# Small steps from VectorE to ScalarE, four trees for k's maximum, and new lists for every queue, in a fused attention and feed-forward kernel

## The chip, the core and the metric

The kernel runs on one core of a Trainium2 chip. A core has TensorE (PE in the profile; its weight loads are PEld), VectorE (DVE), ScalarE (ACT), GpSimd (POOL) and SyncE (SP), each with an instruction queue of its own that it works off in order. An instruction starts when those before it on its engine allow it and the semaphores it waits for are there. Matrix products land in PSUM, in banks that VectorE and ScalarE read (GpSimd doesn't here); all else is in SBUF. Sixteen DMA engines move data; transfers are issued from SP's and POOL's queues, and POOL's are those that convert f32 to f16 on the way.

The metric is the device time of one execution in microseconds (us), the median of several runs.

## The reference

```python
# attention, 8 batches x 8 heads x 576 tokens x 64
q_s = exp(q - max(q, axis=-1));  q_s = q_s / (sum(q_s, axis=-1) + 1e-9)
k_s = exp(k - max(k, axis=2));   k_s = k_s / (sum(k_s, axis=2) + 1e-9)     # axis 2: tokens
kv  = einsum('bhsd,bhse->bhde', k_s, v)
att = einsum('bhsd,bhde->bhse', q_s, kv)
x   = att as (4608, 512)
# feed-forward
out = ((x @ w1) * (x @ w2)) @ w3 @ w_out      # w1, w2: 512x1024; w3: 1024x1024; w_out: 1024x512
```

## The kernel before, in words

**Steps and lists.** The kernel is a set of small named steps, and `Plan.run` (line 48) emits them in the order of one long list, `ORDER` (line 77). Each engine's queue is that list with the other engines' steps left out. A second list, `PICKS`, says for each step that can run on more than one engine which one takes it; `HW`, `LOADS` and `LATE` give the order of the loads from SP, from POOL, and from SP after those. The planner's rings (line 175) are buffers that a step takes and another gives back: `pab` 4 PSUM banks, `po` 2, `att` 2, `osb` 4 and `bsb` 4 in SBUF. `FILL` puts matmuls on zeros before named steps.

`LINKED = 350`: among the first 350 steps, those marked as port steps (the subtractions, the multiplication of q, the trees, some casts; on VectorE or GpSimd) also wait for each other in the order of the list, whenever the engine changes from one to the next.

**Names.** A name's first number is the batch b (for up, bs, ab, down, os and st: the chunk c of 512 tokens; 9 chunks, the last one holding the 64 tokens that each batch leaves over).

- Start: `w3t`, `w3T`, `pf`, `W3O` fold w3 and w_out into one 1024x512 matrix, in 8 parts: transpose on TensorE, copy out (one 1024-column copy), two halves of 4 matmuls each, scaled copy out. w3.0 to w3.3 are loads of one row of w3's blocks, w3.4 and w3.5 of two; wo.0 and wo.1 are w_out's halves. w3t.2 needs w3.2; w3t.4 and w3t.5 need w3.4; w3t.6 and w3t.7 need w3.5.
- k: `kmx` is the maximum over the 9 tokens that a partition holds: two reductions of 1152 elements (line 484), or a tree of four elementwise maxima (lines 493 to 496) in batches below `TREES`. `cb` is the maximum over partitions: a 32x32 transpose, a reduction, an exchange of maxima between neighbouring quarters of 32 partitions (four reductions of 32x8, line 506), a reduction over the pair, a transpose back. `ksub` subtracts, `kexp` takes the exponential (ScalarE).
- `kv`: the products of k and v on TensorE into both `att` banks, with the sum of k's exponentials in a last column. `kv2` adds epsilon to those sums (line 559, once for each of 2 groups), takes the reciprocal, multiplies.
- q, in two parts of 1024 and 1280 elements for a partition: `qmx`, `qsub`, `qexp`, `qsm`, `qeps`, `qrc`, `qn` (maximum, subtract, exponential, sum, epsilon, reciprocal, multiply). Then q is transposed: in batches 0 and 1 on TensorE (`qt`, copied out by `qT`), from batch 2 on by a DMA transpose from SP (`qd`, line 629).
- `xm`, `xt`: q times kv on TensorE (8 of 9 token groups, then the ninth); `xs`, `xts` copy them out. In batches 2 and later xm needs both parts of q.
- Feed-forward: `up.1` (w2) and `up.0` (w1) into a `pab` bank each, 0.87 us; `bs` copies the w2 product to SBUF on ScalarE or VectorE; `ab` multiplies (VectorE), which frees the w1 bank. `down` is 8 matmuls with the folded matrix, 1.73 us, the last ones of which need the last `ab` of their tokens; `os` copies out, `st` stores (two DMAs from SP).

Chunks 0 and 1 are worked in halves of 256 tokens: up.1.c.s.u has the half s and a pair of the 8 blocks of columns u.

Of the kernel before, what the change touches and what calls it, by code (L numbers as in the profile page):

```python
# [77 lines left out]
q.0.1 q.0.0 qmx.0.1 qsub.0.1 w3.3 w3.4 qexp.0.1 qmx.0.0 wo.0 wo.1 k.0 ident qsub.0.0 qexp.0.0 w3t.3  # L78
w3t.4 w3t.5 w3T.3 qsm.0.1 w3T.4 qeps.0.1 qrc.0.1 w3.0 w3.1 pf.3.0 qn.0.1 pf.4.0 qt.0.16 pf.3.1 W3O.3
w3T.5 pf.4.1 qt.0.8 w3.5 v.0 w3.2 q.1.0 qT.0.8 W3O.4 pf.5.0 w3t.0 k.1 w3T.0 pf.5.1 w2.0 W3O.5 w3t.1  # L80
pf.0.0 qT.0.16 w3T.1 pf.0.1 W3O.0 w3t.7 w3T.7 pf.1.0 w3t.6 pf.7.0 pf.1.1 w1.0 qsm.0.0 qeps.0.0
kmx.0.0 cb.0 ksub.0.1 kexp.0.1 w1.1 ksub.0.0 qrc.0.0 kexp.0.0 kv.0 qn.0.0 kv2.0 w3t.2 pf.7.1 qt.0.0
w2.1 qmx.1.0 W3O.1 w3T.6 k.2 W3O.7 w3T.2 pf.6.0 w2.2 qT.0.0 xm.0.0 xs.0.0.1 qsub.1.0 w1.2 qexp.1.0
kmx.1.0 pf.6.1 pf.2.0 pf.2.1 xs.0.0.0 xm.0.1 xs.0.1.0 xs.0.1.1 up.1.0.0.0 up.0.0.0.0 up.1.0.1.0
bs.0.0.0 up.0.0.1.0 up.1.0.0.1 w2.3 qsm.1.0 qeps.1.0 ab.0.0.0 qrc.1.0 w1.3 up.0.0.0.1 cb.1 qn.1.0
v.1 ksub.1.0 q.1.1 ksub.1.1 qt.1.0 W3O.2 bs.0.1.0 ab.0.1.0 up.1.0.1.1 up.0.0.1.1 bs.0.0.1 W3O.6
qT.1.0 bs.0.1.1 ab.0.0.1 q.2 v.2 kmx.2.0 ab.0.1.1 xt.0 kexp.1.0 up.1.0.0.2 bs.0.0.2 up.0.0.0.2
up.1.0.1.2 up.0.0.1.2 kmx.2.1 ab.0.0.2 cb.2 ksub.2.0 ksub.2.1 xts.0.0 xts.0.1 up.1.0.0.3 up.0.0.0.3
# [6 lines left out]
down.0.3 qn.2.1 qT.1.8 xm.1.1 vc.3.0 xs.1.1.1 xs.1.1.0 q.4 down.1.0 qd.2.0 kmx.3.0 qd.2.1 qmx.3.0
xt.1 vc.3.1 up.1.1.1.0 up.0.1.1.0 up.1.1.1.1 bs.1.1.0 up.0.1.1.1 up.1.1.1.2 xts.1.0 bs.1.1.1 os.1.0
xts.1.1 kmx.3.1 ab.1.1.0 os.0.3 qmx.3.1 xm.2.0 qsub.3.0 qmx.4.1 ab.1.1.1 qsub.3.1 qsub.4.1
up.0.1.1.2 down.1.1 xs.2.0.1 bs.1.1.2 k.4 st.0.1 v.5 v.4 st.0.2 xs.2.0.0 xm.2.1 xs.2.1.1 xs.2.1.0
up.1.1.1.3 up.0.1.1.3 up.1.2.0.0 bs.1.1.3 qexp.3.1 ab.1.1.2 cb.3 ksub.3.0 ksub.3.1 up.0.2.0.0
ab.1.1.3 kmx.4.0 bs.2.0.0 qexp.3.0 q.5 qsm.3.1 os.1.1 qexp.4.1 qsm.3.0 qeps.3.0 ab.2.0.0 qeps.3.1  # L100
qrc.3.1 qn.3.1 qd.3.1 st.1.0 qsm.4.1 kexp.3.1 up.1.2.0.1 bs.2.0.1 up.0.2.0.1 down.1.2 down.1.3
os.1.3 up.1.2.0.2 up.0.2.0.2 bs.2.0.2 qrc.3.0 ab.2.0.1 qn.3.0 kexp.3.0 up.1.2.0.3 ab.2.0.2
up.0.2.0.3 kmx.4.1 bs.2.0.3 kv.3 qd.3.0 up.1.2.0.4 ab.2.0.3 up.0.2.0.4 vc.5.0 vc.5.1 vc.4.1 vc.4.0
k.5 st.1.3 st.0.3 st.1.1 v.6 v.7 bs.2.0.4 kv2.3 os.1.2 up.1.2.0.5 ab.2.0.4 st.1.2 up.0.2.0.5
bs.2.0.5 qmx.4.0 xt.2 xm.3.1 xts.2.0 up.1.2.0.6 xts.2.1 ab.2.0.5 qsub.4.0 xs.3.1.1 xm.3.0 bs.2.0.6
xt.3 up.0.2.0.6 xts.3.1 xs.3.0.0 cb.4 up.1.2.0.7 xts.3.0 xs.3.0.1 up.0.2.0.7 xs.3.1.0 bs.2.0.7
ab.2.0.6 up.1.3.0.0 ksub.4.0 qexp.4.0 ab.2.0.7 down.2.0 kmx.5.1 bs.3.0.0 down.2.1 ksub.4.1 kexp.4.0
qmx.5.1 up.0.3.0.0 os.2.0 up.1.3.0.1 qsub.5.1 kexp.4.1 ab.3.0.0 down.2.2 qmx.5.0 bs.3.0.1 kmx.5.0
qsub.5.0 up.0.3.0.1 qeps.4.1 up.1.3.0.2 up.0.3.0.2 qrc.4.1 os.2.1 ab.3.0.1 qn.4.1 up.1.3.0.3 qsm.4.0
k.6 st.2.1 down.2.3 bs.3.0.2 qeps.4.0 ab.3.0.2 qexp.5.1 qd.4.1 up.0.3.0.3 qrc.4.0 qn.4.0 bs.3.0.3  # L110
st.2.0 up.1.3.0.4 qsm.5.1 kv.4 bs.3.0.4 ab.3.0.3 up.0.3.0.4 qd.4.0 qexp.5.0 os.2.2 up.1.3.0.5
ab.3.0.4 q.6 st.2.2 up.0.3.0.5 kv2.4 bs.3.0.5 qeps.5.1 up.1.3.0.6 os.2.3 qrc.5.1 ab.3.0.5 qn.5.1
up.0.3.0.6 st.2.3 bs.3.0.6 xm.4.0 ab.3.0.6 xm.4.1 xs.4.0.0 xt.4 up.1.3.0.7 xs.4.1.1 up.0.3.0.7
xs.4.1.0 bs.3.0.7 xs.4.0.1 ab.3.0.7 down.3.0 cb.5 down.3.1 os.3.0 xts.4.1 st.3.0 xts.4.0 kmx.6.0
ksub.5.0 up.1.4.0.0 os.3.1 down.3.2 bs.4.0.0 st.3.1 q.7 kmx.6.1 ksub.5.1 qd.5.1 up.0.4.0.0 kexp.5.0
up.1.4.0.1 qsm.5.0 up.0.4.0.1 bs.4.0.1 ab.4.0.0 qeps.5.0 up.1.4.0.2 kexp.5.1 ab.4.0.1 up.0.4.0.2
qrc.5.0 bs.4.0.2 qmx.6.1 qn.5.0 up.1.4.0.3 os.3.2 vc.6.0 up.0.4.0.3 st.3.2 ab.4.0.2 up.1.4.0.4
qmx.6.0 bs.4.0.3 qd.5.0 k.7 kv.5 bs.4.0.4 ab.4.0.3 qsub.6.0 up.0.4.0.4 vc.6.1 kv2.5 up.1.4.0.5
# [5 lines left out]
os.4.1 qrc.6.0 kv.6 ab.5.0.2 qn.6.0 xt.5 up.1.5.0.3 qsm.7.0 xts.5.0 os.4.2 up.0.5.0.3 xts.5.1
kmx.7.0 qsub.7.1 bs.5.0.3 qd.6.0 up.1.5.0.4 up.0.5.0.4 st.4.1 bs.5.0.4 ab.5.0.3 up.1.5.0.5 ab.5.0.4
st.4.0 up.0.5.0.5 bs.5.0.5 kv2.6 up.1.5.0.6 st.4.2 ab.5.0.5 xm.6.0 bs.5.0.6 xm.6.1 st.3.3 xt.6
up.0.5.0.6 xs.6.1.1 cb.7 xts.6.1 xts.6.0 up.1.5.0.7 xs.6.1.0 xs.6.0.0 up.0.5.0.7 xs.6.0.1 ab.5.0.6
down.4.3 ksub.7.1 qexp.7.1 bs.5.0.7 ab.5.0.7 up.1.6.0.0 os.4.3 qsm.7.1 vc.7.1 down.5.0 ksub.7.0
bs.6.0.0 qeps.7.1 up.0.6.0.0 qrc.7.1 up.1.6.0.1 ab.6.0.0 kexp.7.0 down.5.1 os.5.0 qeps.7.0 st.5.0
# [12 lines left out]
st.7.1 ab.8.0.5 up.0.8.0.6 bs.8.0.6 st.5.3 down.7.2 ab.8.0.6 st.6.3 up.1.8.0.7 up.0.8.0.7 os.7.2
bs.8.0.7 st.7.2 down.7.3 ab.8.0.7 down.8.0 os.7.3 st.7.3 down.8.1 os.8.0 st.8.0 down.8.2 os.8.1
st.8.1 down.8.3.0 os.8.2 down.8.3 st.8.2 os.8.3.0 st.8.3.0 os.8.3 st.8.3
# [764 lines left out]
```

## Time and profile before

| | us |
|---|---|
| median of 3 runs (lowest, highest) | 242.14 (242.06, 242.51) |
| the profiled execution | 242.07 |
| its span | 240.3 |
| TensorE busy | 232.4 |
| VectorE busy | 182.0 |
| ScalarE busy | 118.5 |
| GpSimd busy | 110.2 |
| first matmul of up | 34.58 |
| last matmul of TensorE ends | 237.0 |

The span is what the profile covers; 1.8 us of the execution lie outside it. TensorE's 232.4 us hold 9.2 us of matmuls on zeros. Busy us of each engine by stretch, from the trace:

| stretch | PE | DVE | ACT | POOL |
|---|---|---|---|---|
| 0 to 30 | 26.6 | 20.7 | 14.5 | 15.4 |
| 30 to 60 | 28.8 | 28.2 | 18.1 | 21.0 |
| 60 to 80 | 20.0 | 18.7 | 15.1 | 15.8 |
| 80 to 100 | 20.0 | 19.2 | 15.1 | 15.6 |
| 100 to 120 | 20.0 | 17.0 | 10.8 | 12.2 |
| 120 to 140 | 20.0 | 18.8 | 10.8 | 13.4 |
| 140 to 160 | 20.0 | 19.3 | 11.5 | 10.9 |
| 160 to 180 | 20.0 | 14.5 | 10.7 | 6.1 |
| 180 to the end | 57.0 | 25.7 | 11.9 | 0.0 |

A group of instructions in the profile has: line, engine, operation, what it writes and reads, count, busy us and mean ns of one, then the idle time of the engine just before them and who ended it. A row of the timeline has start, length, and in brackets the idle time before it.

### The profile page before, as it was taken

To read this page: it belongs to the slowest core of one execution; us is meant where nothing else is said; L and a number is where in the kernel's file an instruction comes from. 1 tells how busy PE (TensorE), PEld (TensorE's weight loads), DVE (VectorE), ACT (ScalarE), POOL (GpSimd) and SP (SyncE) were. 2 spreads that over 40 slices of the span, in tenths; PEclk is the share of its full clock that TensorE was granted. 3 is DMA by queue.
4 is the path that set the end of the run, shared out by engine and by line. 5 is a ranking of instruction groups with operands and counts; after the bars stand their busy time and mean duration, and the time that the engine had idled before them with its cause. 6 is when DMAs were issued, how large, how long until landed. Compare 5 with 4: busy or idle time off the path is not lost.

```text
span 240.3 us, 4954 instructions
## 1 busy us (share of the span) xinstructions
PE 232.4 (97%) x1987; PEld 121.0 (50%) x1987; DVE 182.0 (76%) x306; ACT 118.5 (49%) x187; POOL 110.2 (46%) x73
## 2 busy tenths in 40 slices
...
PEclk9999999999999999999999999999999999999999
...
GB/s 203 217 305 209 324 222 296 235 393 391 314 261 277 402 217 194 323 372 284 206 232 213 260 125 0 57 151 68 65 124 87 46 0 0 0 132 1 131 131 131
DMA packets 37894, 45.66 MB, mean 190 GB/s; under 512 B 15984, under 2 KB 22384, under 8 KB 37872
## 3 DMA queue, kind: packets, MB, share of 16 engines
...
q8 instruction: 15, 0.25, 0.4%
q14 instruction: 7, 0.06, 0.1%
...
## 4 chain that ended last, share of the span: by engine, by line
PE 83%; DVE 6%; DMA 6%; issue 2%; POOL 1%; ACT 1%; DVEq 0%; POOLq 0%
PE pab L768 50%; PE po L790 23%; DMA k<-in_k_dram 6%; PE po L805 3%; PE pkv L540 2%; PE po L452 2%; PE xm L654 2%; DVE ab L783 1%; DVE k L515 1%; DVE km L484 1%; PE qtp L621 1%; POOL w L402 1%; PE po L654 1%; DVE mx L506 1%; DVE kmx L493 1%
## 5 line engine op out<-in xcount | busy, mean ns | idle before, releaser
L783 DVE TENSOR_TENSOR ab<-pab,bsb 128x512 f16<-128x512 f32 x72 | 48.7, 682 | 24.0 <-PE pab L768 19.7
L768 PE MATMUL pab<-x,w2sb 128*128 128x512 f16 (+1 forms) x320 | 66.0, 337 | 0.0
L768 PE MATMUL pab<-x,w1sb 128*128 128x512 f16 (+1 forms) x320 | 65.9, 337 | 0.0
L323 ACT CAST bsb<-pab 128x512 f16<-128x512 f32 x59 | 34.5, 587 | 54.3 <-PE pab L768 53.9
L790 PE MATMUL po<-W3O,ab 128*128 128x512 f16 x256 | 59.7, 379 | 1.2 <-DVE ab L783 1.2
L768 PEld LDWEIGHTS <-w1sb 128*128 128x128 f16 x352 | 33.9, 98 | 27.6 <-DMA w1sb<-in_moe_w_dram 0.2
L768 PEld LDWEIGHTS <-w2sb 128*128 128x128 f16 x352 | 33.4, 98 | 27.6 <-issue 1.3
L790 PEld LDWEIGHTS <-ab 128*128 128x128 f16 x256 | 24.7, 98 | 30.6 <-DVE ab L783 1.9
L515 POOL TENSOR_TENSOR k<-k,cb 128x1152 f32<-128x1152 f32 x12 | 31.4, 2636 | 14.9 <-DVE cb L511 8.4
L574 POOL TENSOR_TENSOR q<-q,qm 128x1024 f32<-128x1024 f32 (+1 forms) x14 | 29.7, 2125 | 12.8 <-DVE qm L569 12.7
L606 POOL TENSOR_TENSOR en<-eq,qr 128x1280 f16<-128x1280 f16 (+1 forms) x12 | 25.8, 2159 | 20.7 <-DVE qr L599 20.7
L484 DVE TENSOR_REDUCE km<-k 128x128 f32<-128x1152 f32 x12 | 25.9, 2166 | 0.0
L569 DVE TENSOR_REDUCE qm<-q 128x20 f32<-128x1280 f32 (+1 forms) x16 | 21.3, 1342 | 3.6 <-DMA q<-in_q_dram 3.6
L523 ACT ACTIVATE ek<-k 128x1152 f16<-128x1152 f32 x16 | 18.5, 1163 | 9.5 <-POOL k L515 8.8
L323 ACT COPY osb<-po 128x512 f32<-128x512 f32 (+1 forms) x22 | 12.7, 576 | 20.6 <-PE po L790 14.1
L323 DVE COPY osb<-po 128x512 f32<-128x512 f32 (+1 forms) x15 | 10.0, 668 | 15.4 <-PE po L790 9.7
L587 DVE TENSOR_REDUCE qr<-eq 128x20 f32<-128x1280 f16 (+1 forms) x16 | 21.3, 1341 | 0.5 <-ACT eq L582 0.5
L582 ACT ACTIVATE eq<-q 128x1280 f16<-128x1280 f32 (+1 forms) x16 | 18.8, 1174 | 5.6 <-POOL q L574 3.8
L452 PE MATMUL po<-wosb,w3T 128*128 128x512 f16 x64 | 15.5, 379 | 0.7 <-DMA wosb<-in_moe_w_out_dram 0.4
L327 ACT ACTIVATE x<-xm 128x512 f16<-128x512 f32 x18 | 10.4, 608 | 4.6 <-PE xm L654 4.6
L323 DVE CAST bsb<-pab 128x512 f16<-128x512 f32 x13 | 8.9, 687 | 2.8 <-PE pab L768 2.3
L350 PE MATMUL po<-zero 128*128 128x512 f16 x31 | 9.2, 458 | 1.6 <-DVE zero L345 1.6
...
## 6 DMA issues: line engine op xcount, KB each, us to landing
...
```

Source lines behind the costliest of these rows:

```text
L323: return [(nc.scalar.copy if eng == "ACT" else engine[eng].tensor_copy)(out=out, in_=in_)]
L452: nc.tensor.matmul(st["pf", ft], lhsT=st["w3T", ft][:, gt, :], rhs=wosb[:, gt, :], start=(gt == 0), stop=(gt == N_FT - 1))
L484: dve.tensor_reduce(out=st["km", b][:, two(hp), :], in_=kb[:, two(hp), :, :].rearrange("p h j d -> p h d j"), axis=AX.X, op=ALU.max)
L515: return [engine[eng].tensor_tensor(out=kb[:, two(hp), :, :], in0=kb[:, two(hp), :, :], in1=st["cb", b][:, two(hp), None, :].broadcast_to( ...
L569: dve.tensor_reduce(out=st["qm", b][:, :, j], in_=qb[:, :, j, :], axis=AX.X, op=ALU.max)
L574: return [engine[eng].tensor_tensor(out=qb[:, :, j, :], in0=qb[:, :, j, :], in1=st["qm", b][:, :, j, None].broadcast_to([P, HH, n, D]), op ...
L582: nc.scalar.activation(out=st["eq", b, p], in_=qb[:, :, j, :], func=AF.Exp)
L587: dve.tensor_reduce(out=st["qr", b][:, :, slice(*PARTS[p])], in_=st["eq", b, p], axis=AX.X, op=ALU.add)
L606: return [engine[eng].tensor_tensor(out=st["en", b][:, j, :, :].rearrange("p j h d -> p h j d"), in0=st["eq", b, p], in1=st["qr", b][:, :, ...
L768: nc.tensor.matmul(st["p", one, c, sub, u][:, a * (t1 - t0):(a + 1) * (t1 - t0)], lhsT=w[:, ct, fb * P:(fb + 1) * P], rhs=x()[:, ct, t0:t1 ...
L783: dve.tensor_tensor(out=st["ab", c][:, nf * u:nf * u + nf, t0:t1], in0=cut(st["p", 0, c, sub, u]), in1=cut(st["bsb", c, sub, u]), op=ALU.mult)
L790: nc.tensor.matmul(st["po", c, tb], lhsT=st["ab", c][:, ft, tb * P:(tb + 1) * P], rhs=W3O[:, ft, :], start=(ft == 0), stop=(ft == N_FT - 1))
```

## The change

Four things are changed together.

1. The exchange between quarters, in all 8 batches, becomes a step of its own on ScalarE. `cb` is split in three: `cba` (VectorE: transpose, reduction), `cbx` (ScalarE: four copies of 32x8), `cb` (VectorE: reduction, transpose).
2. The addition of epsilon to k's sums becomes a step `kve` on ScalarE (two activations of 128x2, from PSUM); `kv2` keeps the reciprocal and the products.
3. `TREES` goes from 2 to 4: batches 2 and 3 take the tree for kmx too, which is a port step.
4. `ORDER`, `PICKS`, `FILL`, `HW`, `LOADS` and `LATE` are new throughout: nearly every queue's order differs.

Steps by engine that differ in number, before and after:

| step | VectorE | ScalarE | GpSimd |
|---|---|---|---|
| bs | 13, 21 | 59, 51 | |
| os | 15, 9 | 22, 28 | |
| W3O | 0, 3 | 8, 5 | |
| w3T | 2, 3 | 6, 5 | |
| xs | 7, 6 | 25, 26 | |
| xts | 4, 5 | 12, 11 | |
| ksub | 4, 6 | | 12, 10 |
| qsub | 2, 3 | | 14, 13 |
| qn | 4, 3 | | 12, 13 |
| vc (cast of v) | | 6, 5 | 6, 7 |

```diff
-    TREES = 2
+    TREES = 4
...
-        def cb():
+        def cba():
             t = work.tile([P, nq, QD], F32, tag="kmq", name="kmq")
             dve.transpose(out=t.rearrange("p n c -> p (n c)"),
                           in_=st["km", b].rearrange("p h d -> p (h d)"))
-            m = work.tile([P, nq, 2], F32, tag="mx", name="mx")
-            dve.tensor_reduce(out=m[:, :, 0], in_=t, axis=AX.X, op=ALU.max)
+            st["mx", b] = work.tile([P, nq, 2], F32, tag="mx", name="mx")
+            dve.tensor_reduce(out=st["mx", b][:, :, 0], in_=t, axis=AX.X, op=ALU.max)
+
+        def cbx():
+            m = st["mx", b]
             for x in range(P // QD):
                 y = x ^ 1
-                dve.tensor_reduce(out=m[x * QD:(x + 1) * QD, :, 1],
-                                  in_=m[y * QD:(y + 1) * QD, :, 0:1], axis=AX.X, op=ALU.max)
+                nc.scalar.copy(out=m[x * QD:(x + 1) * QD, :, 1], in_=m[y * QD:(y + 1) * QD, :, 0])
+
+        def cb():
             e = work.tile([P, nq], F32, tag="mxe", name="mxe")
-            dve.tensor_reduce(out=e, in_=m, axis=AX.X, op=ALU.max)
+            dve.tensor_reduce(out=e, in_=st["mx", b], axis=AX.X, op=ALU.max)
...
+        def kve():
+            st["rc", b] = work.tile([P, G, NHP], F32, tag="rc", name="rc")
+            for gg in range(G):
+                nc.scalar.activation(out=st["rc", b][:, gg, :], in_=st["pkv", b, gg][:, :, D],
+                                     func=AF.Identity, bias=epst[:, 0:1])
+
         def kv2():
...
-            rc = work.tile([P, G, NHP], F32, tag="rc", name="rc")
-            for gg in range(G):
-                dve.tensor_scalar_add(out=rc[:, gg, :], in0=ps[gg][:, :, D], scalar1=EPS)
+            rc = st["rc", b]
             dve.reciprocal(out=rc, in_=rc)
...
-    "begin": 17, "w3t.4": 8, "pf.3.0": 6,
+    "begin": 17, "w3t.4": 8, "qt.0.0": 7,
...
-    ("q", 0, 1), ("q", 0, 0),
+    ("q", 0, 0), ("q", 0, 1),
...
-    ("w3", 3), ("w3", 4), ("wo", 0), ("wo", 1), ("k", 0), ("w3", 0), ("w3", 1), ("w3", 5), ("v",
-    0), ("w3", 2), ("q", 1, 0), ("k", 1), ("w2", 0), ("w1", 0), ("w1", 1), ("w2", 1), ("k", 2),
-    ("w2", 2), ("w1", 2), ("w2", 3), ("w1", 3), ("v", 1), ("q", 1, 1),
+    ("w3", 0), ("w3", 4), ("wo", 0), ("wo", 1), ("w3", 2), ("k", 0), ("w3", 5), ("w3", 3),
+    ("w3", 1), ("v", 0), ("q", 1, 0), ("k", 1), ("w2", 0), ("w1", 0), ("w2", 1), ("w1", 1),
+    ("w2", 3), ("w1", 2), ("w2", 2), ("k", 2), ("w1", 3), ("v", 1), ("q", 1, 1),
```

The new `ORDER` up to the end of batch 2's attention, without the steps before kv.0 on TensorE that the prediction names one by one:

```
w3t.7 w3t.6 w2.0 w1.0 w3t.3 w2.1 w1.1 cbx.0 W3O.2 w3T.7 w2.3 w1.2 w2.2 qT.0.8 qT.0.16 cb.0 pf.7.0 pf.7.1
ksub.0.1 ksub.0.0 w3T.3 pf.3.0 pf.3.1 kexp.0.1 w3t.1 kexp.0.0 k.2 kv.0 W3O.3 w3T.1 W3O.7 w3T.6 qmx.1.0
kve.0 kv2.0 pf.1.0 pf.6.0 xm.0.0 qsub.1.0 xs.0.0.0 xs.0.0.1 pf.6.1 pf.1.1 kmx.1.0 xm.0.1 qexp.1.0
...
bs.0.0.3 ab.0.0.3 down.0.0 xts.0.0 kexp.1.1 cba.2 ab.0.1.2 xts.0.1 cbx.2 cb.2 ksub.2.1 kv.1 kve.1
bs.0.1.3 kexp.2.1 os.0.0 down.0.1 ksub.2.0 v.2 up.0.0.1.3 kv2.1 qmx.1.1 xm.1.0 xs.1.0.0 xs.1.0.1 qsub.1.1
ab.0.1.3 down.0.2 up.1.1.0.0 up.0.1.0.0
...
up.0.1.0.2 kv.2 kve.2 ab.1.0.1 up.1.1.0.3 up.0.1.0.3 qn.1.1 qrc.2.0 kv2.2 qn.2.0 qeps.2.1 qt.1.16 qt.1.8
os.0.3 ab.1.0.2 bs.1.0.3 qrc.2.1 qn.2.1 st.0.0 k.4 qd.2.0 ab.1.0.3 qT.1.16 down.1.0 qmx.3.1 qT.1.8 qd.2.1
q.4 st.0.1 xm.1.1 down.1.1 xs.1.1.1 xs.1.1.0 xt.1 kmx.3.0 qmx.3.0 up.1.1.1.0 up.0.1.1.0 xts.1.1 xts.1.0 xm.2.0
```

More of the change, by code (lines that the diff above doesn't have):

```diff
@@ L77 @@
 ORDER = """
[L78 to L88, printed above, removed]
@@ L95 @@
[L95 to L106, printed above, removed]
@@ L107 @@
[L107 to L118, printed above, removed]
@@ L124 @@
[L124 to L129, printed above, removed]
@@ L142 @@
[L142 to L144 removed]
+q.0.0 q.0.1 w3.0 ident qmx.0.0 qsub.0.0 w3.4 wo.0 wo.1 w3.2 k.0 qmx.0.1 w3.5 w3.3 qexp.0.0 qsm.0.0
+qsub.0.1 w3t.0 qeps.0.0 w3t.4 qrc.0.0 w3t.5 w3T.0 w3.1 qn.0.0 qexp.0.1 w3T.5 qsm.0.1 qeps.0.1
+qrc.0.1 qn.0.1 qt.0.0 pf.0.0 pf.5.0 pf.0.1 w3t.2 pf.5.1 W3O.0 qT.0.0 v.0 kmx.0.0 q.1.0 k.1 cba.0
@@ new lines @@
+w3T.2 W3O.5 qt.0.8 qt.0.16 pf.2.0 pf.2.1 w3T.4 pf.4.0 pf.4.1 W3O.4 w3t.7 w3t.6 w2.0 w1.0 w3t.3 w2.1
+w1.1 cbx.0 W3O.2 w3T.7 w2.3 w1.2 w2.2 qT.0.8 qT.0.16 cb.0 pf.7.0 pf.7.1 ksub.0.1 ksub.0.0 w3T.3
+pf.3.0 pf.3.1 kexp.0.1 w3t.1 kexp.0.0 k.2 kv.0 W3O.3 w3T.1 W3O.7 w3T.6 qmx.1.0 kve.0 kv2.0 pf.1.0
+pf.6.0 xm.0.0 qsub.1.0 xs.0.0.0 xs.0.0.1 pf.6.1 pf.1.1 kmx.1.0 xm.0.1 qexp.1.0 xs.0.1.1 xs.0.1.0
+up.1.0.0.0 bs.0.0.0 up.0.0.0.0 up.1.0.1.0 up.0.0.1.0 up.1.0.0.1 qsm.1.0 qeps.1.0 qrc.1.0 ab.0.0.0
+cba.1 w1.3 v.1 q.1.1 qn.1.0 bs.0.1.0 up.0.0.0.1 qt.1.0 ab.0.1.0 up.1.0.1.1 up.0.0.1.1 cbx.1 cb.1
```

100 lines of the change are left out of this document (68 added, 32 removed), and 100 rows, old and new, of the table PICKS.

## The prediction

> **What bounds the kernel now.** I read the engine shares first, then what TensorE waited for, then its timeline around its longest wait, then the timelines of the loads and of VectorE beside it. From the page and from TensorE's waits:
>
> ```profile
> PE 232.4 (97%) x1987; PEld 121.0 (50%) x1987; DVE 182.0 (76%) x306; ACT 118.5 (49%) x187; POOL 110.2 (46%) x73
> ...
> PEclk9999999999999999999999999999999999999999
> ```
>
> ```profile
> PE po L350 <- DVE zero L345: 1.6, 1, 1.6
> PE po L790 <- DVE ab L783: 1.2, 1, 1.2
> PE w3t L440 <- DMA w<-in_moe_w_dram: 0.7, 2, 0.5
> ```
>
> TensorE is busy 97% at full clock, and its waits are few. The timeline (start, length, idle before) shows where:
>
> ```profile
> 12.67 1.89 PE L452 MATMUL po<-wosb,w3T 128*128 128x512 f16 x8
> ...
> 34.58 1.05 PE L768 MATMUL pab<-x,w2sb 128*128 128x256 f16 x8
> ...
> 50.37 0.60 PE L790 MATMUL po<-W3O,ab 128*128 128x512 f16 x2 [1.23 <-DVE ab L783]
> ...
> 229.90 7.09 PE L805 MATMUL po<-W3O,ab 128*128 128x512 f16 x40
> ```
>
> After 52 us there is no gap to 237.0; only what lies before 52 us can be won, and any new gap after it is a loss. Two things time that first part. One is the loads:
>
> ```profile
> 15.04 1.89 PE L452 MATMUL po<-wosb,w3T 128*128 128x512 f16 x8 [0.36 <-DMA wosb<-in_moe_w_out_dram]
> ...
> 18.02 1.23 DVE L493 TENSOR_TENSOR kmx<-k 128x1024 f32<-128x1024 f32 x1 [2.94 <-DMA k<-in_k_dram]
> ...
> 19.14 0.71 PE L440 MATMUL w3t<-ident,w 128*128 128x128 f16 x8 [0.46 <-DMA w<-in_moe_w_dram]
> ```
>
> They land one behind the other: k.0 3.0 us after wo.1, the next one-row part of w3 1.1 us after k.0. The other is VectorE, 85 to 100% busy in each 6 us from 30 to 60 us. The prices that the change turns on, from the groups of instructions:
>
> ```profile
> L484 DVE TENSOR_REDUCE km<-k 128x128 f32<-128x1152 f32 x12 | 25.9, 2166 | 0.0
> ...
> L506 DVE TENSOR_REDUCE mx<-mx 32x8 f32<-32x8 f32 x32 | 4.9, 153 | 0.6
> ...
> L559 DVE TENSOR_SCALAR rc<-pkv 128x2 f32<-128x2 f32 x16 | 1.7, 150 | 1.8 <-PE pkv L550 1.8
> ...
> L593 ACT ACTIVATE qr<-qr,epst 128x16 f32<-128x16 f32 x5 | 1.5, 310 | 2.9 <-DVE qr L587 2.9
> ```
>
> (busy us, mean ns, idle before). And from the view of L629, the DMA transposes of q:
>
> ```profile
> DMA to landing us min/median/max: 3.1/3.6/7.4
> ```
>
> **The change, part by part.** All times are of the one profiled execution: span 240.3 us, 242.07 us in all, 1.8 us outside the span; the median of the three runs is 242.14.
>
> *Loads off VectorE.* The 32 copies at L506 leave it (4.9 us), and the 16 additions at L559 (1.7). Batches 2 and 3 exchange four reductions (4 x 2.17) for two trees (1.23 + 0.69 + 0.42 + 0.43 and small gaps, 2.9 each): 2.9 less. The new lists give back eight bs, three W3O, one w3T, one xts, one qsub and two ksub and take six os, one xs and one qn: +6.3. Net 3 us less on VectorE, spread over the attention.
>
> *Loads on ScalarE.* Four copies of 32x8 for each batch and two additions of 128x2. An ACT copy takes 372 ns at 256 columns and 586 at 512, so about 165 at 8; two of the small L593 activations stand in 0.52 us where they follow each other. I take 0.75 us for the four copies (bounds 0.6, the same on VectorE, and 1.24, four times L593) and 0.55 for the two additions (0.23, the two at L559, to 0.62). With fewer bs, W3O, w3T, vc and more os ScalarE gets about 5 us more, on an engine that is half idle. The cost is the hop: cb was 2.3 us in one go and is now 0.9 + 0.75 + 0.65 with two handovers, and cbx stands in ScalarE's queue between evictions. Queued behind a cbx that waits for its cba are, batch by batch, W3O.2 (pf.7 waits for its bank), qT.1.0, kve.1, xs.2.1.1, xts.2.1, kve.4, bs.4.0.1 (ab.4.0.1 and up.0.4.0.3 wait for it) and bs.5.0.0.
>
> *Start.* POOL issues w3.0, the identity, w3.4, wo.0, wo.1, w3.2 and only then k.0. The DMA queues have q to move meanwhile, so the identity's 0.6 us costs nothing; w3.2 costs k.0 the 1.2 us of one part, so it lands at 19.25. The qsub that held POOL's later issues in the old order is on VectorE now; since the queues were never empty, that gains nothing. Fills are 32 for 31 (0.2 us, inside the wait for qn.0.0 and wo.0). Walking the queues: tree 19.25 to 22.1; cba 23.0; cbx 23.8; cb 24.5; two ksub 27.1; kexp.0.0 28.4; kv.0 28.45. TensorE, with w3t.2 at 16.3 (w3.2), w3t.7/6 at 21.75 (w3.5), pf.7 at 24.35 (behind W3O.2, which is behind cbx.0), reaches kv.0 at 28.45 as well: one more w3t, half a pf and a qt now lie before kv.0 (27.11 in the old order, after a wait of 0.4). From there 5.6 us are left: kv 1.25, pf.1 and pf.6 3.46, two xm with the gaps before them 0.9. kve (29.8 to 30.4, behind w3T.6) and kv2 (31.15) hide behind the two pf, to 31.4. So up.1.0.0.0 starts at about 34.05 instead of 34.58: **-0.5 us**.
>
> *Chunk 0.* VectorE is the chain here. From kv2.0 (31.15): qsub, tree, qsm and two small ones to 36.85; ab, cba.1, ab 39.0; cb.1 39.9 (0.25 wait for cbx.1); bs, ksub, ab, bs, ab, W3O, ab 44.9; tree of batch 2 47.7 (k.2 was moved behind all w2 and lands at 43.1; POOL's ksub.1.1, which the port order puts first, ends at 44.5); ab.0.0.3 48.35. TensorE needs that ab for the last two of the eight matmuls of down.0.0 at 48.9: the 1.23 us of the old order are gone. Next: cba.2, ab, cb.2 50.7 (0.2 wait for cbx.2), ksub.2.1 52.05, bs, kv2.1 53.4, qmx, ab.0.1.3 55.45. TensorE has put down.0.1 and up.0.0.1.3 before that; down.0.2 waits 0.35 for ab.0.1.3 and ends at 55.9. The old order has the same work done at 56.09 + 1.73 = 57.8. **-1.4, so -1.9 together.**
>
> *Batch 2.* Here it is given back. POOL's chain starts at the end of ksub.2.1, since the port order makes ksub.2.0 wait for it: 2.64 + 2.34 + 2.34 + 1.91 + 1.15 + 2.34 + 1.91 + 2.34 with small gaps, so qn.2.1 ends at 69.45, which is when it ended before. The transposes land 3.6 us later: 73.1. The old order reached xm.2.0 at 74.8 and didn't wait; the new one has less work ahead of it, comes at about 72.4 and waits 0.7. Before that up.0.1.0.3 waits 0.35 for ab.1.0.1. With xm.2.0 done at 73.45, the same work was done at 74.25 before (74.82, less 0.55 of work listed ahead of it there and not here): **+1.1, leaving -0.8**.
>
> *Rest.* The tree of batch 3 (69.75 to 72.6) ties POOL's vc.3.1 and qsub.3.0 behind it, which still leaves ksub.3.1 done at 83.2 for kv.3 at 86.8. Chunk 2 has up.1.3.0.0 at 98.55 against 99.27. From there VectorE is nearly full to 142 us, with margins of 0.3 to 1.1 us (down.3.0 needs ab.3.0.7 at 124.6, up.1.5.0.0 needs xs.5.0.0 at 142.6 and comes at 143.7). The POOL steps listed between up.1.3.0.0 and up.1.5.0.0 were 29 us by their rows and are 44 now, in the same 45 us; POOL begins them 4.8 us early; kv.5 and kv.6 have 8 us and more. Stores moved past q.6 and k.6 on SP still free osb before the os that need it. Allowing 0.1 for these: **-0.7 in all**. The last steps are the same (a 256-column ACT copy and a store).
>
> 242.07 - 0.7 = **241.4 us**.
>
> **Rivals.** (a) *The transposes of batch 2 land late.* Twelve of them took 3.1 to 7.4 us. POOL's chain ends no earlier than before while TensorE comes 2.4 us earlier, so each us over 3.6 is one us of the end. At 4.8 us it is slower than before by 0.5; at 7.4 it gives 245.2; 5.5, the middle, 243.3. For it: k.4 and q.4 load around them. Against it: the median. (b) *Small ScalarE steps cost 0.31 each*, as L593 does. cbx becomes 1.24, and cbx.0 lies on both ways to kv.0: +0.5, then 241.9, no change. Against it: the copy rows' 158 ns at no columns. The Trainium skill, ScalarE: Activation LUTs, Rules for kernel authors, speaks for (b): it budgets about 0.3 us for each ACTIVATE with a pointer bias besides the elements. L593 agrees at 310 ns; whether a plain copy pays it no row here shows. By the rule for copies too the sum would be 241.9. (c) *VectorE overruns in chunks 3 and 4.* I priced back-to-back steps at 0.09 less than their means (two ab in 1.28); if half of that is missing over some 60 steps, 2.7 us less 1.1 of margin come on top: 243.0. For it: no idle time in that list. (d) *The waits close up.* If VectorE and POOL run 1.5 us ahead of my walk, both waits vanish: 239.9. Against it: POOL's chain has no slack.
>
> **How the numbers follow.** From no change a measurement of this kernel can tell about 0.2%, 0.5 us, that is 241.66 to 242.62. Forecast 0.42 (of which 0.06 within 0.2%), (a) 0.20, (b) 0.14, (c) 0.12, (d) 0.12. Faster 0.36 + 0.12 = 0.48; same 0.06 + 0.14 = 0.20; slower 0.32. The range runs from 240.2, which cuts half of (d), to 243.3, which cuts half of (a) and a quarter of (c), 0.19 in all; the forecast's own is 240.9 to 241.9.
>
> **What would show it.** Right: first L768 matmul near 34.0; no wait of 1.2 us for ab at the first down; TensorE waits 0.5 to 1 us before the xm of batch 2 near 73; ACT copies of 32x8 near 0.17 us each; nothing after 100 us. Wrong: kv.0 later than 29, the gap near 73 over 2 us, or gaps on ab between 100 and 145.

## The result, and the profile after

The changed kernel takes 244.04 us (median of 4 runs, 243.87 to 244.72) against 242.27 (4 runs, 242.06 to 242.51) for the kernel before: a ratio of 1.0078, with a 95% interval of 1.0055 to 1.0101. It is slower by 1.8 us; 241.4 was forecast, and 243.3 was the upper end of the range. Its profiled execution took 244.17 us, with a span of 242.4.

Engine shares and granted clock, from the page of the kernel after:

```profile
PE 232.4 (96%) x1988; PEld 121.3 (50%) x1988; DVE 179.7 (74%) x270; ACT 123.1 (51%) x228; POOL 106.3 (44%) x72
...
PEclk9999999999999999999999999999999999999998
```

The loads moved between engines as costed: VectorE 2.3 us less (3 forecast), ScalarE 4.6 more (5 forecast). TensorE's work is the same; the last slice's 8 lies behind its last matmul. So the 2.1 us by which the span is longer are waiting, 0.7 of them behind TensorE's last matmul. Everything TensorE waited for, from the view of waits of the kernel after (total us, times, longest):

```profile
PE po L350 <- DVE zero L345: 1.6, 1, 1.6
PE po L662 <- DMA qT<-en: 1.2, 1, 1.2
PE w3t L440 <- DMA w<-in_moe_w_dram: 1.2, 3, 0.6
PE xm L662 <- DMA qT<-en: 0.6, 1, 0.6
PE po L452 <- ACT w3T L323: 0.5, 1, 0.5
PE pab L779 <- DVE bsb L323: 0.3, 1, 0.3
PE pab L779 <- DVE ab L794: 0.2, 1, 0.2
```

The wait for ab at the first down is gone; two waits for DMA transposes and two for VectorE are new. TensorE's timeline of the kernel after shows their places:

```profile
22.43 1.97 PE L440 MATMUL w3t<-ident,w 128*128 128x128 f16 x24 [0.32 <-DMA w<-in_moe_w_dram]
...
26.66 1.90 PE L452 MATMUL po<-wosb,w3T 128*128 128x512 f16 x8 [0.54 <-ACT w3T L323]
28.40 0.65 PE L440 MATMUL w3t<-ident,w 128*128 128x128 f16 x8
28.98 0.78 PE L544 MATMUL pkv<-v,ek 64*64 64x64 f16 x72
...
34.58 1.05 PE L779 MATMUL pab<-x,w2sb 128*128 128x256 f16 x8
...
48.43 1.89 PE L801 MATMUL po<-W3O,ab 128*128 128x512 f16 x8
...
73.37 0.41 PE L662 MATMUL xm<-qT,kv 64*64 64x512 f16 x4 [0.62 <-DMA qT<-en]
...
97.57 0.41 PE L662 MATMUL po<-qT,kv 64*64 64x512 f16 x4 [1.23 <-DMA qT<-en]
...
156.13 1.02 PE L779 MATMUL pab<-x,w2sb 128*128 128x512 f16 x4 [0.35 <-DVE bsb L323]
157.33 1.02 PE L779 MATMUL pab<-x,w1sb 128*128 128x512 f16 x4 [0.17 <-DVE ab L794]
...
231.25 7.09 PE L816 MATMUL po<-W3O,ab 128*128 128x512 f16 x40
```

The same work, after minus before: up.1.0.0.0 0.0 (34.58 both); end of down.0.2 -1.5 (56.28, 57.82); up.1.2.0.0 -0.6 (79.41, 79.97); up.1.3.0.0 +0.7 (99.93, 99.27); batch 5's first xm +0.6 (140.42, 139.86); batch 6's first xm +1.3 (162.60, 161.26); last down +1.35 (231.25, 229.90); end of the span +2.1. The kernel is ahead until 79 us, loses 1.2 us at batch 3's xm, 0.8 us near 156, and the rest behind the last matmul. The prices of the moved steps, from the groups of instructions of the kernel after:

```profile
L509 ACT COPY mx<-mx 32x8 f32<-32x8 f32 x32 | 6.3, 197 | 4.8 <-DVE mx L503 4.4
...
L561 ACT ACTIVATE rc<-pkv,epst 128x2 f32<-128x2 f32 x16 | 3.3, 259 | 4.3 <-PE pab L662 2.0 <-PE pkv L554 1.2 <-PE pkv L544 1.0
```

And who makes batch 3's transposes late. VectorE, GpSimd and SyncE's queue, from the timelines of the kernel after:

```profile
84.34 1.48 DVE L577 TENSOR_REDUCE qm<-q 128x20 f32<-128x1280 f32 x1
85.73 2.17 DVE L484 TENSOR_REDUCE km<-k 128x128 f32<-128x1152 f32 x1
87.83 0.26 DVE L607 RECIPROCAL qr<-qr 128x20 f32<-128x20 f32 x1
```

```profile
83.25 1.15 POOL L323 CAST v<-v 128x1152 f16<-128x1152 f32 x1
85.95 2.34 POOL L582 TENSOR_TENSOR q<-q,qm 128x1280 f32<-128x1280 f32 x1 [1.55 <-issue]
88.25 4.21 POOL L614 TENSOR_TENSOR en<-eq,qr 128x1280 f16<-128x1280 f16 x2
```

```profile
90.62 1.28 SPq L637 DMA_TRANSPOSE qT<-en  x1
91.99 1.36 SPq L827 DMA_DIRECT2D out_dram<-osb  x2
93.44 1.34 SPq L637 DMA_TRANSPOSE qT<-en  x1
```

qrc.3.1 stands on VectorE behind kmx.4.0 and runs at 87.83; GpSimd has idled 1.55 us (qsub.4.1 needs qmx.4.1, which ends on VectorE at 85.82) and then does qsub.4.1, for batch 4, ahead of batch 3's qn.3.1 and qn.3.0, which end at 92.46; two stores are issued between the two transposes. The kernel before began qn.3.1 at 86.56, 1.7 us sooner, and issued its first transpose at 88.92; two stores stood between the two transposes there too.

### The profile page after: what moved, and what is told of

It is laid out like the page before. It is cut to its first block, busy times and chain, and to the rows that moved or that the text cites. A ratio compares the mean times of both kernels' runs of the same rounds, so it can differ in the third digit from the quotient of the medians.

```text
span 242.4 us, 4971 instructions
## 1 busy us (share of the span) xinstructions
PE 232.4 (96%) x1988; PEld 121.3 (50%) x1988; DVE 179.7 (74%) x270; ACT 123.1 (51%) x228; POOL 106.3 (44%) x72
## 4 chain that ended last, share of the span: by engine, by line
PE 50%; DVE 18%; DMA 9%; issue 7%; ACT 7%; POOL 6%; DVEq 0%; ACTq 0%; POOLq 0%
PE pab L779 30%; PE po L801 13%; DMA k<-in_k_dram 6%; DVE ab L794 5%; DMA qT<-en 3%; PE po L816 3%; POOL en L614 2%; PE po L452 2%; DVE qr L595 2%; ACT eq L590 2%; DVE qm L577 2%; DVE k L519 2%; ACT mx L509 2%; POOL q L582 1%; ACT bsb L323 1%
## 5 line engine op out<-in xcount | busy, mean ns | idle before, releaser
L519 POOL TENSOR_TENSOR k<-k,cb 128x1152 f32<-128x1152 f32 x10 | 26.2, 2633 | 13.5 <-DVE k L519 10.4
L614 POOL TENSOR_TENSOR en<-eq,qr 128x1024 f16<-128x1024 f16 (+1 forms) x13 | 27.2, 2106 | 4.4 <-issue 1.2
L582 POOL TENSOR_TENSOR q<-q,qm 128x1280 f32<-128x1280 f32 (+1 forms) x13 | 27.7, 2143 | 2.6 <-issue 1.6
L577 DVE TENSOR_REDUCE qm<-q 128x16 f32<-128x1024 f32 (+1 forms) x16 | 21.2, 1336 | 3.5 <-DMA q<-in_q_dram 3.5
L595 DVE TENSOR_REDUCE qr<-eq 128x16 f32<-128x1024 f16 (+1 forms) x16 | 21.2, 1330 | 2.0 <-ACT eq L590 2.0
L590 ACT ACTIVATE eq<-q 128x1024 f16<-128x1024 f32 (+1 forms) x16 | 18.5, 1164 | 3.7 <-POOL q L582 2.2
L323 DVE CAST bsb<-pab 128x512 f16<-128x512 f32 x21 | 14.4, 687 | 3.9 <-PE pab L779 3.3
L484 DVE TENSOR_REDUCE km<-k 128x128 f32<-128x1152 f32 x8 | 17.2, 2154 | 0.0
L323 DVE COPY osb<-po 128x512 f32<-128x512 f32 x9 | 6.2, 685 | 7.2 <-PE po L801 7.2
L323 POOL CAST v<-v 128x1152 f16<-128x1152 f32 x7 | 9.2, 1314 | 4.1 <-DVE km L496 3.0
```

The costliest lines, as they stand in the source:

```text
L323: return [(nc.scalar.copy if eng == "ACT" else engine[eng].tensor_copy)(out=out, in_=in_)]
L519: return [engine[eng].tensor_tensor(out=kb[:, two(hp), :, :], in0=kb[:, two(hp), :, :], in1=st["cb", b][:, two(hp), None, :].broadcast_to( ...
L577: dve.tensor_reduce(out=st["qm", b][:, :, j], in_=qb[:, :, j, :], axis=AX.X, op=ALU.max)
L582: return [engine[eng].tensor_tensor(out=qb[:, :, j, :], in0=qb[:, :, j, :], in1=st["qm", b][:, :, j, None].broadcast_to([P, HH, n, D]), op ...
L590: nc.scalar.activation(out=st["eq", b, p], in_=qb[:, :, j, :], func=AF.Exp)
L595: dve.tensor_reduce(out=st["qr", b][:, :, slice(*PARTS[p])], in_=st["eq", b, p], axis=AX.X, op=ALU.add)
```

## Experiments

Each was timed beside the kernel before on the same chip (its medians were 242.12 to 242.30 there).

**Code without lists, lists without code.** Where a kernel has fewer or more steps than its list had, `LINKED` is set so that the same stretch stays tied.

The exchange and the epsilon on ScalarE, in the old lists:

```diff
-... cb.0 ...        kv2.0 ...          (the lists of the kernel before, TREES = 2)
+... cba.0 cbx.0 cb.0 ...  kve.0 kv2.0 ...
```

> The kernel before with its own lists; only the code of the change is in it: the exchange between quarters as cba, cbx (ScalarE), cb at the place of cb, and the epsilon as kve (ScalarE) ahead of kv2. No new trees, no new order. Theory A (the new lists lose the time: the transposes of batches 2 and 3 come late, 0.62 and 1.23 us, and VectorE is full at 155, 0.52 us): the steps alone cost only their handoffs, 242.0 to 243.0. Rival B (the handoffs of the split steps lose it: each batch's exchange becomes 0.2 to 0.5 us longer, each kv2 0.3 us): 243.3 to 244.5, with gaps on TensorE ahead of up.1.0.0.0 and the middle products.

Measured 251.56 us, ratio 1.0389 (1.0375 to 1.0403): above the ranges of both theories. ScalarE's timeline of this kernel:

```profile
22.86 0.60 ACT L329 ACTIVATE W3O<-po 128x512 f16<-128x512 f32 x1 [0.39 <-PE po L454]
23.57 1.01 ACT L325 COPY w3T<-w3t 128x1024 f16<-128x1024 f16 x1
24.61 0.82 ACT L511 COPY mx<-mx 32x8 f32<-32x8 f32 x4
```

cba.0 was done at 21.74, but cbx.0 started at 24.61: it stood behind evictions that the old list had put before cb.0 when that was VectorE's step. TensorE then waited 3.46 us for kexp.0 and its clock fell for some 5 us (last section); up.1.0.0.0 came at 39.69 in place of 34.58. That is 5.1 of the 9.4 us; the others follow in later waits of 0.3 to 1.6 us. So at this place the price of the moved step is its position in the other queue, not the hop of a few tenths.

The trees alone, in the old lists:

```diff
-    TREES = 2
+    TREES = 4                # and kmx.2.1, kmx.3.1 left out of the old list
```

> The kernel before with its own lists and steps; only the trees for k's maxima of batches 2 and 3, at the places of kmx.2.0 and kmx.3.0, with their tie to POOL on the shared port. Theory A: a tree measured 2.85 us against two reductions of 2.17 us each, so VectorE loses 1.5 us near 45 and near 70; the gap of 1.23 us at the first down may shrink, nothing else moves: 241.3 to 242.4. Rival C (a tree holds POOL's chain of batch 3 back by its port tie, as the 2.97 us of POOL's idle time ahead of v's cast at 72.8 suggest): over 242.8, with a wait for transposes of batch 2 or 3 at xm.

Measured 246.90 us, ratio 1.0196 (1.0176 to 1.0216). The time is rival C's, the place isn't: it is batch 2's tree. VectorE's timeline, then TensorE's, of this kernel:

```profile
46.55 1.23 DVE L493 TENSOR_TENSOR kmx<-k 128x1024 f32<-128x1024 f32 x1 [5.12 <-POOL k L515]
```

```profile
50.08 1.87 PE L768 MATMUL pab<-x,w2sb 128*128 128x256 f16 x8 [3.84 <-DVE ab L783]
```

VectorE, tied, waits 5.12 us for GpSimd's two subtractions, and TensorE 3.84 us behind it. Is it the tie or the tree?

```diff
-            A(("kmx", b, 0), {"DVE": (2.85, True)}, 0, kmx_tree, [("k", b)])
+            A(("kmx", b, 0), {"DVE": (2.85, b < 2)}, 0, kmx_tree, [("k", b)])
```

> As the run with the trees alone in the old lists (246.9, VectorE idle for 5.12 us ahead of the tree of batch 2, TensorE for 3.84 us behind it), but the trees of batches 2 and 3 are not tied to POOL on the port. If the tie, and not the tree, is the price: 241.4 to 243.0, the 5.12 us gone, the tree no longer than 3.3 us. If trees themselves are slow beside POOL's work (they share the port): a tree of 4 us or more, and 243.5 to 247.

Measured 247.68 us, ratio 1.0217 (1.0203 to 1.0230). VectorE's timeline without the tie:

```profile
41.43 6.26 DVE L493 TENSOR_TENSOR kmx<-k 128x1024 f32<-128x1024 f32 x1
...
47.73 0.69 DVE L494 TENSOR_TENSOR kmx<-kmx 128x512 f32<-128x512 f32 x1
```

The second theory's mechanism, and a little above its 247 us. The same instruction takes 6.26 us in place of 1.23: it is done only 1.1 us after the end of GpSimd's second subtraction (43.98 to 46.61), and TensorE waits 4.58 us. So the tie only writes down a wait that comes without it too. The two reductions at that place in the kernel before took 2.17 us each beside the same GpSimd rows. A tree saves 1.5 us of VectorE only where GpSimd's queue leaves it the port; in the new list it stands behind ksub.1.1.

The converse, with the new lists and trees and both pieces back on VectorE, and with the exchange alone back:

```diff
-... cba.0 ... cbx.0 ... cb.0 ... kve.0 ... kv2.0      (the lists of the kernel after)
+... cb.0 ...                           ... kv2.0      # second kernel: kve.0 stays
```

> The lists and trees of the kernel after, with the exchange and the epsilon back on VectorE (cb as one step at the place of cba, kv2 with its two adds). Theory A: the lists carry the loss, 243.6 to 244.8: the waits for the transposes near 73 and 97 stay, VectorE has about 3 us more to do. Rival B (the split steps lose it): 242.0 to 243.2.

> The kernel after with the exchange back on VectorE as one step cb at the place of cba; the epsilon stays on ScalarE. It tells the two moved pieces apart: with both back the time was 246.1. If the exchange (0.65 us of VectorE a batch) is what the new lists live on: 245.2 to 246.1; if the epsilon ahead of kv2 is: 244.0 to 244.8.

Measured 246.09 us (1.0163, 1.0149 to 1.0177) and 245.40 us (1.0127, 1.0112 to 1.0143). TensorE's waits in the first of them:

```profile
PE xt L653 <- DVE kv L561: 1.2, 1, 1.2
PE po L789 <- DVE ab L782: 1.0, 2, 0.9
...
PE xm L653 <- DMA qT<-en: 0.5, 1, 0.5
```

The first lies above both theories, the second in the range of its first theory. In the new lists the moved steps earn 2.0 us, 1.4 of it the exchange and 0.7 the epsilon: without them VectorE, busy 38.6 of the 40 us from 60 to 100 (37.2 in the kernel after), delays kv2 and ab. So the steps don't make the loss, they lessen it. But theory A is only half borne out: TensorE still waits for batch 2's transposes, and no longer for batch 3's, because it comes later.

The new lists with reductions in place of the two new trees:

```diff
-    TREES = 4
+    TREES = 2                # kmx.2.1, kmx.3.1 follow kmx.2.0, kmx.3.0
```

> The kernel after with its own lists, but k's maxima of batches 2 and 3 by two reductions each again, at the places of the trees and without their tie to POOL. Theory T (trees belong to the gain: 2 times 2.15 us against 2.8 us, so VectorE has 1.5 us more to do near 45 and near 70, where it is already the busy engine): 244.8 to 246.5, with the gap at the first down back and a later qsub.3.0. Rival C (the tie of kmx.3.0 to POOL, 2.97 us of idle POOL ahead of v's cast at 72.8, is what makes batch 3's transposes late): 242.6 to 243.6, the wait of 1.23 us at xm.3.1 shrinks by a microsecond.

Measured 245.82 us, ratio 1.0153 (1.0131 to 1.0175): theory T by the time, though only 0.16 us of the gap at the first down came back. The trees earn 1.8 us here. GpSimd, free of the tie, waited even longer at that place, 4.04 us in place of 2.97, for qmx.3.0 behind the reductions; batch 3's wait grew to 1.75. (This trace is of an execution of 247.26 us, the slowest of the five, so the 1.8 us rest on the medians.)

**Which places lose it.** One cast moved, in the kernel after:

```diff
-    "bs_5_0_2": "DVE"
+    "bs_5_0_2": "ACT"
```

> The kernel after with one cast, bs.5.0.2, on ScalarE (idle from 153.8 to 155.7) and not on VectorE. If VectorE's full stage causes the two gaps near 156 and 157 (0.35 and 0.17 us), both go and the time is 243.4 to 243.7; if they only close up into later ones, 243.9 to 244.2.

Measured 243.04 us, ratio 1.0044 (1.0026 to 1.0063): 1.0 us better than the kernel after, more than the first theory gave. Both gaps are gone and none came later. From batch 5's first xm to batch 6's TensorE needs 21.4 us, as in the kernel before; in the kernel after it was 22.2. TensorE's last down starts 0.64 sooner; the rest of the microsecond lies behind it (below).

Batch 3's queries first, a blunt reordering:

```diff
-... kexp.3.1 ... qeps.3.1 qeps.3.0 kmx.4.0 qsub.4.1 qexp.4.1 ... qrc.3.1 ... qrc.3.0 ... qsm.4.1 ... qn.3.1 ... qn.3.0 qsub.4.0
+... qeps.3.1 qeps.3.0 kexp.3.1 ... qrc.3.1 qrc.3.0 qn.3.1 qn.3.0 kmx.4.0 ... qsub.4.1 qsub.4.0 ... qexp.4.1 ... qsm.4.1
```

> The kernel after with one stretch reordered: on ScalarE qeps.3.1 and qeps.3.0 ahead of kexp.3.1, on VectorE qrc.3.1 and qrc.3.0 ahead of kmx.4.0, on POOL qn.3.1 and qn.3.0 ahead of qsub.4.1 (with qexp.4.1 and qsm.4.1 moved behind). Theory A: qn.3.0 ends about 2 us sooner, the transposes land ahead of xm.3.1 and its wait of 1.23 us goes; 242.6 to 243.1. Rival D (the wait only closes up: later waits, for VectorE or for batch 4's transposes, take it over): 243.6 to 244.2, with new gaps between 98 and 135.

Measured 245.07 us, ratio 1.0120 (1.0106 to 1.0134): worse than both theories. Batch 3's wait fell from 1.23 to 0.27, but ab then came 1.19 us late at 98.2 and batch 4's transposes 0.75 us late at 115.5, since batch 4's steps had been pushed back on engines without slack. The gentler form gives batch 4 its place back by running qmx.4.1 earlier:

```diff
-... qsm.3.1 ab.2.0.1 qmx.4.1 ... os.1.1 ... qeps.3.1 qeps.3.0 kmx.4.0 qsub.4.1 ... qrc.3.1 qmx.4.0 ... qn.3.1 ... qn.3.0
+... qmx.4.1 qsub.4.1 ab.2.0.1 qsm.3.1 ... qeps.3.1 qeps.3.0 os.1.1 ... qmx.4.0 qrc.3.1 qrc.3.0 qn.3.1 qn.3.0 kmx.4.0 ...
```

> The kernel after with the stretch from 82 to 92 reordered so that batch 3's queries end earlier and batch 4's do not end later: on VectorE qmx.4.1 ahead of qsm.3.1 and qrc.3.1, qrc.3.0 ahead of kmx.4.0; on POOL qsub.4.1 can then start at 84.4 in place of 85.95, and qn.3.1, qn.3.0 follow at once; on ScalarE qeps.3.* ahead of os.1.1. Theory A: qn.3.0 ends near 91.4 in place of 92.46, the wait of 1.23 us at xm.3.1 falls to 0.1 to 0.4: 242.9 to 243.4. Rival D (a slack moved is a wait elsewhere, as in the first reordering): 243.7 to 245, with a new gap on ab or on batch 4's transposes.

Measured 243.83 us, ratio 1.0059 (1.0047 to 1.0071): almost no gain. The time is rival D's, but no new gap came. qn.3.0 ended at 90.98, 1.5 us sooner, but its transposes were issued at 91.97, behind two stores, and xm.3.1 started at 96.99, 0.6 us sooner, while TensorE had come 0.5 us sooner too: it still waited 1.14. So the stores were moved alone, in the kernel after:

```diff
-... qd.3.1 st.1.1 qd.3.0 ...
+... qd.3.1 qd.3.0 st.1.1 ...
```

> The kernel after with one edit: the stores st.1.1 stand behind qd.3.0 in SyncE's queue. In after qn.3.0 ended at 92.46 and its transposes were issued only at 93.44, behind the two stores that were issued from 91.99. If that place in the queue is most of the wait of 1.23 us: the wait falls to 0.1 to 0.5 us and 243.0 to 243.5. If POOL's chain or the DMA engines set the landing: 243.8 to 244.2.

Measured 243.93 us, ratio 1.0070 (1.0057 to 1.0083): the second theory's range. The second transpose was issued at 92.2 in place of 93.44, but the wait is still 1.04 us: xm.3.1 started 4.9 us after that issue in place of 4.1, with the DMA engines busy 85 to 92% from 91 to 97. Counted from the issue of the first transpose it started 6.8 us later, 6.95 in the kernel after, and 7.8 in the kernel before this one, where the first was issued sooner and the second still stood behind the stores. So neither edit alone pays: not the place in SyncE's queue, not the earlier chain. Together, with the moved cast:

```diff
-    "bs_5_0_2": "DVE"
+    "bs_5_0_2": "ACT"
 ... and the stretch from qmx.4.1 to kmx.4.0 as two kernels above ...
-... qd.3.1 st.1.1 qd.3.0 ...
+... qd.3.1 qd.3.0 st.1.1 ...
```

> The kernel after with the cast bs.5.0.2 on ScalarE, the stretch from 82 to 92 reordered as in the run before (qn.3.0 then ends at 91.0), and the stores st.1.1 put behind the transposes qd.3.0 in SyncE's queue. If SyncE's queue holds the transposes back (in the run before qn.3.0 ended at 90.98 and the transposes were issued at 91.97, behind two stores): landing near 96, the wait at xm.3.1 0.1 to 0.5, and 242.0 to 242.6. If the DMA engines, which were 99% busy there, set the landing: the wait stays near 1.1 and 242.7 to 243.1.

Measured 242.80 us, ratio 1.0024 (1.0015 to 1.0033). The wait at xm.3.1 is gone, as the first theory had it, though the time lies in the second's range. From up.1.2.0.0 to up.1.3.0.0 TensorE needs 19.2 us (20.5 in the kernel after, 20.4 and 20.3 with one of the two edits, 19.3 in the kernel before). SyncE's queue in this kernel, where the row in the kernel after was two rows with the stores between:

```profile
89.19 3.10 SPq L637 DMA_TRANSPOSE qT<-en  x2
92.38 1.18 SPq L827 DMA_DIRECT2D out_dram<-osb  x2
```

But beside the kernel with the moved cast alone (243.04) the time is only 0.24 us better. A new wait for batch 4's transposes shows, which the earlier one had covered:

```profile
113.61 0.41 PE L662 MATMUL xm<-qT,kv 64*64 64x512 f16 x4 [0.64 <-DMA qT<-en]
```

From up.1.3.0.0 to batch 5's first xm TensorE now needs 41.8 us, in the kernel after 40.5: batch 4 takes back 1.3 us. The wait for batch 3 had closed up into the next one. Two places around 70 us:

```diff
-... xs.1.1.1(DVE) ... kmx.3.0 qmx.3.0 ... xm.2.0 bs.1.1.0 xs.2.0.0 xs.2.0.1 cba.3 ab.1.1.0 up.1.1.1.1
+... xs.1.1.1(ACT) ... qmx.3.0 kmx.3.0 ... bs.1.1.0 cba.3 ab.1.1.0 up.1.1.1.1 xm.2.0 xs.2.0.0 xs.2.0.1
```

> As the run with three edits, and around 70: xs.1.1.1 on ScalarE, qmx.3.0 ahead of the tree kmx.3.0 (VectorE then works where it waited for POOL), and xm.2.0 behind up.1.1.1.1, so that its transposes have landed. Each wait has its own cause: the 0.62 us at xm.2.0 goes, VectorE's chain to batch 3 comes 0.7 us sooner: 241.3 to 242.2, at or below the kernel before. If the waits only close up: no better than the run with three edits.

Measured 242.43 us, ratio 1.0003 (0.9989 to 1.0017): level with the kernel before, 0.2 above what was expected, with 0.30 us for ab at 79.9 and 0.47 and 0.22 us at batch 4's xm left. In the traces TensorE's last down starts no sooner than with three edits (230.26, 230.16); the gain lies behind it, so these two places are not shown to have earned anything alone. VectorE's timeline of this kernel shows what holds batch 4's queries up:

```profile
99.84 1.16 DVE L595 TENSOR_REDUCE qr<-eq 128x16 f32<-128x1024 f16 x1
101.04 1.54 DVE L603 TENSOR_SCALAR qr<-qr 128x16 f32<-128x16 f32 x1
```

An addition on 16 columns, qeps.4.0, takes 1.54 us beside GpSimd's subtractions (100.19 to 104.4); the same operation took 0.17 in the kernel before. It ends at 102.58, when the first of the two subtractions does (102.53): the port again, past step 350 where nothing is tied. Its reciprocal, qrc.4.0, then stands behind a reduction of 2.15 us. The last kernel:

```diff
-    "qeps_4_0": "DVE"
+    "qeps_4_0": "ACT"
-... qsm.4.0 qeps.4.0 kexp.4.0 bs.3.0.0 ... ab.3.0.0 kmx.5.1 qrc.4.0 ...   os.1.0 cbx.3
+... qsm.4.0 kexp.4.0 bs.3.0.0 qeps.4.0 ... ab.3.0.0 qrc.4.0 kmx.5.1 ...   cbx.3 os.1.0
```

> As the run with five edits, and two more places: qeps.4.0 on ScalarE with qrc.4.0 ahead of kmx.5.1 (in the run before the qeps.4.0 of 16 elements took 1.54 us on VectorE beside POOL's subtractions, and batch 4's scaling on POOL began 1.1 us late), and the copy os.1.0 behind cbx.3 on ScalarE, so that cb.3 and the reduction behind it start 0.6 us sooner. If every wait is a place in a queue: the waits near 79.9 and 113.6 go (0.3, 0.47 and 0.22 us), 241.3 to 241.9, faster than the kernel before. If a rest belongs to the split steps and the trees: new waits take their place and 242.2 to 242.8.

Measured 241.22 us, ratio 0.9965 (0.9952 to 0.9978): faster than the kernel before by 0.35%, and than the kernel after by 2.8 us. From up.1.3.0.0 to batch 5's first xm it is 40.6 us again. All that TensorE still waits for, from its waits:

```profile
PE po L350 <- DVE zero L345: 1.6, 1, 1.6
PE w3t L440 <- DMA w<-in_moe_w_dram: 0.8, 2, 0.5
PE po L452 <- ACT w3T L323: 0.3, 1, 0.3
PE xt L662 <- ACT mx L509: 0.2, 1, 0.2
```

All four parts of the change are still in it. So the loss doesn't belong to the split steps or the trees: it lay in a few places of the new lists. Which of the seven edits could be left out was not tried.

## Why the prediction was wrong

**Loads: right.** VectorE -2.3 us, ScalarE +4.6. The four copies of cbx took 0.82 to 0.83 us (0.75 taken), 197 ns each by the mean, and the two additions 0.40 to 0.43 (0.55 taken). Rival (b)'s 0.31 for each copy fell. The Trainium skill, ScalarE: Activation LUTs, Rules for kernel authors, budgets about 0.3 us for each ACTIVATE with a pointer bias; L561's 259 ns are a little less than that, and a plain copy doesn't pay it here.

**Start, -0.5: 0.0 in the two profiled executions, about -0.4 by the traces of other kernels.** up.1.0.0.0 came at 34.58 in both. But in the eight other kernels with the same new start it came at 34.23 to 34.41, and in the two others with the old start at 34.81 and 34.90: the means, with this pair, are 34.35 and 34.76. So the term was nearly right, and this pair shows none of it; the 34.05 of the walk came nowhere. The walk had k.0's chain and TensorE reach kv.0 together at 28.45. In the kernel after kv.0 came at 28.98 (28.63 to 28.81 in the eight) with no wait ahead of it: TensorE was the later of the two. w3t.7 ran at 22.43 in place of 21.75, waiting for w3.5, and the fold behind it waited 0.54 us for w3T.3, which stands behind qT.0.8 on ScalarE; the walk left that out. k.0's tree started 0.25 late, 19.50.

**Chunk 0, -1.4: right.** The wait of 1.23 us is gone, and down.0.2 ends 1.54 us earlier than the same work before, at 56.28 (55.9 forecast, the start's error included). Its wait of 0.35 didn't come.

**Batch 2, +1.1: right.** GpSimd's qn.2.1 ended at 69.80 (69.45), the transposes came at 73.37 (73.1), the wait was 0.62 (0.7). Rival (a) had the right kind of wait at the wrong batch, and only part of its cause: batch 3's first transpose was issued 1.7 us later than before (90.62, 88.92), and xm.3.1 then started 6.95 us after it, where 6.04 were enough before.

**Rest, +0.1: this is the step that failed.** For batch 3 it followed the tie of the tree to ksub.3.1, 83.2 (83.31 measured), and to kv.3, and stopped there. The other half of the batch, q through qrc.3.1 on VectorE, qn.3.* on GpSimd and two transposes, was not walked: the 0.1 allowed for all that follows batch 2 had no row behind it, and it measured +1.2 at batch 3 and +0.8 near 156. Its last transpose came at 97.57, and TensorE waited 1.23 us; up.1.3.0.0 came at 99.93, not 98.55. The runs show that no single place in that stretch sets it. The earlier chain on ScalarE, VectorE and GpSimd, moved as one, and SyncE's stores take 0.1 and 0.2 us off the stage alone and 1.3 together. But with batch 3's wait gone batch 4 took 1.3 us back; only the last kernel's edits removed that.

**Nothing after 100 us: half right.** From 100 to 140 TensorE was busy 40.0 of 40 us, so rival (c) fell where it was put. But the margins were followed to 142 us only. Near 156 VectorE, busy 19.4 of the 20 us from 140 to 160, was late: 0.52 us of waits, 0.8 us of the stage, and one cast moved to ScalarE, idle then, won all of it back. Part of VectorE's lateness is a price that the costing lacked: it gave two more of k's subtractions to VectorE without a wait for the port. The second of batch 7's two ran beside a cast of GpSimd, and it stands on the chain that ended last in the kernel after (start, length, what); GpSimd's timeline beside it:

```profile
150.27 2.30 DVE k L519
```

```profile
149.06 2.30 POOL L323 CAST v<-v 128x1152 f16<-128x1152 f32 x1 [1.14 <-DMA v<-in_v_dram]
```

Elsewhere they take 1.36 and 1.15 us. No run takes this away by itself; with the moved cast VectorE had room for it. None of the three signs of being wrong that were named came (kv.0 later than 29, over 2 us near 73, gaps on ab between 100 and 145): the loss lay where the walk had not gone.

**Tail, the same: not quite.** From TensorE's last matmul to the end of the span there were 3.3 us before and 4.1 after (242.4 - 231.25 - 7.09), with the same last copy and store. Other kernels of this case showed 3.3 or 3.4 (the one with the trees alone, the one with five edits, the one with seven) or 3.6 to 4.3 (no new trees, the moved cast, batch 3 pulled up). The order of the last steps doesn't set it: it is the same in the kernel with batch 3's queries first (3.3) and in the one with batch 3 pulled up (4.3). SyncE's last wait for a store was 1.5 us in place of 0.7; why, the traces don't show. This stays open; it is 0.7 us of the 2.1 between the two profiled executions, and the medians are 1.8 apart.

The sum in the terms of the prediction: forecast -0.5 - 1.4 + 1.1 + 0.1 = -0.7; measured 0.0 - 1.5 + 1.0 + 1.2 (batch 3) + 0.7 (156 us and after) + 0.7 (tail) = +2.1 for the profiled execution.
